# Decay sums of a gated linear attention: one matmul for each of two matrices, against two half-row matmuls with both matrices side by side

## The chip, the cores and the metric

The kernel runs on one core of a Trainium2 chip. The metric is the device time in microseconds (us) of one execution. The engines' names in the profile: PE is TensorE (its weight loads are listed as PEld and overlap its matmuls), DVE is VectorE, ACT is ScalarE, POOL is GpSimd, SP is SyncE, which issues most DMAs.

## The reference

A complex gated linear attention (4 batches, 8 heads, 768 tokens, head size 48) feeds a maxout FFN (model size 384 = 8 x 48, inner size 768) over 3072 tokens.

```python
mag = sqrt(a_re*a_re + a_im*a_im)
scale = minimum(mag, 0.999) / (mag + 1e-6)        # the gate is a*scale: a decay and an angle
for t in range(768):                              # per batch, head
    S = (a_re + 1j*a_im)[t][:, None] * scale[t][:, None] * S + outer(k[t], v[t])
    y[t] = real(q[t] @ S)
x = y as [3072, 384]
out = maximum(maximum(x @ w1, x @ w2), x @ w3) @ w_out
```

The weights arrive as 64-bit floats, everything else as 32-bit floats.

## The kernel before

**Tiles.** The tokens are cut into 24 tiles `x` of 128 tokens, each of two chunks of 64, and 12 groups `g` of two tiles. A tile holds tokens on partitions and the 384 = 8 x 48 channels in columns.

**Decay sums.** `gate_steps` makes `Ln`, minus the logarithm of the clipped magnitude, for each token and channel. `products(x)` needs two sums of it over tokens, both as matmuls with a constant 128x128 matrix of 0, 1 and -1 as stationary operand. `mid` gives each token the signed sum between it and the middle of its block of eight tokens; its entries are nonzero only inside blocks of eight. `rest` gives the sum from that block's middle to the end of the 64-token chunk; it is nonzero only inside a chunk, so both matrices are block-diagonal in 64x64 blocks. The steps of `products`:

- `s0`: the matmul `mds` (L405, PSUM), then E = exp(+mds) and E = exp(-mds) on ACT (L106), multiplied into `k` and `q` (L415; on DVE for the first two groups, on POOL after that).
- `s1`: `k` and `q` times cosine and sine give `Uk` and `Uq` (L420, DVE).
- `s2`, listed as `kt` in `tile_steps`: the matmul `sfx` (L405), En = exp(-sfx) on ACT, and `Uk` times En (L428, DVE). This `Uk` is used for the state update alone.

**The rest of a tile.** `turn` transposes Uk and Uq (`tp`, L442; copies to `K` and `Q` on ACT, L444 and L446). `cut` makes `F`, eight matmuls of a head's 48 channels with 74 columns (L455), and exponentiates it into `f` (ACT, L106). `prep` multiplies `K` and `Q` by columns of `f` into Q's factors, `KB`, `QB` and `QG` (L469, DVE). `scores` makes `A` (L504) and `B` (L507), `gather` copies them by mask into `atm` (L516), `state` makes `dk` (L548) and the running state `g`, `outputs` makes `y` (L576), copied to `xT` (L584). The angles of a group come from `turns`: an arctan (ACT, behind a table load at L109), w times ar and plus ai (L355 and L356, DVE), and the running sums `cs` (PE, L360 and L362).

**The FFN.** `up_step` makes 256 inner channels with one of three weights (`up`, L598). The first is copied to `hT` by ACT (L601), the other two go into `hT` by a maximum on DVE (L603). `out_step` makes `op` (L609).

**PSUM.** `tp`, `F`, `mds`, `sfx`, `cs`, `up`, `y` and `op` share one pool `psM` of four buffers, given out in turn. A matmul therefore waits until the fourth buffer before it has been read.

**Order.** Each engine executes its instructions in program order. `weave` merges lists of steps by fractions of a group: the steps of two tiles, the preparation of the next group (`gate_steps`, both tiles' `s0`, the angles, both tiles' `s1`) and the FFN steps of the tokens that are done. So `s0` of the next group, `mds` in the profile, stands between up steps, and `s2` of the next tile stands before `outputs` of the present one. The steady part is groups 2 and later, from about 180 us on.

**The start.** Constants are made by selects on POOL (`keep`, L120) in `constants_early`, ahead of the first group's gates, and `constants_late`, behind its angles. The weights are loaded as 64-bit words and turned into 32-bit floats by `weight_round` (L284 to L292, DVE and ACT), three rounds before the first angles, the others woven into the first group.

Of the kernel before, what the change touches and what calls it, by code (L numbers as in the profile page):

```python
# [9 lines left out]
FP = mybir.dt.float32  # L10
# [3 lines left out]
AF = mybir.ActivationFunctionType  # L14
OP = mybir.AluOpType
# [30 lines left out]
def kernel(  # L46
# [13 lines left out]
    nc = tc.nc  # L60
    B, H, S, D = q.shape
    P = 128
    L64 = 64
    DD = L64 + D
    DM = H * D
# [23 lines left out]
    nat2 = ctx.enter_context(tc.tile_pool(name="nat2", bufs=2))  # L89
# [4 lines left out]
    psM = ctx.enter_context(tc.tile_pool(name="psM", bufs=4, space=PSUM))  # L94

    T = {}
    order = mybir.DependencyInfo(mybir.DependencyClass.NoSync, mybir.DependencyReason.DATA)

    def tab(ins):

        if "tab" in T:
            tc.add_manual_dep(ins.ins, T["tab"].ins.name, order, reason="table order")
        T["tab"] = ins

    def act(**kw):
        tab(nc.scalar.activation(**kw))  # L106
# [11 lines left out]
    def keep(view, base, pattern, mult):  # L118

        nc.gpsimd.affine_select(out=view, in_=view, compare_op=OP.is_ge, fill=0.0, base=base,  # L120
                                pattern=pattern, channel_multiplier=mult)

    def ones(name, *shape):
        t = const.tile([P, *shape], FP, name=name)
        nc.vector.memset(t, 1.0)
        return t

    def between(view, low, high, lp, hp):

        keep(view, -low - 1, [[-s, n] for s, n in lp], 1)  # L130
        keep(view, high, [[s, n] for s, n in hp], -1)
# [2 lines left out]

    upto = ones("upto", P)

    mid = ones("mid", P)

    rest = ones("rest", P)

    cuts = ones("cuts", NF)

# [11 lines left out]
    fs = [const.tile([P, H, NF], FP, name="f%d" % i) for i in range(2)]  # L154

    def constants_early():
        halves = mid.rearrange("p (n u h) -> p n u h", u=2, h=4)
        left, right = halves[:, :, 0], halves[:, :, 1]
        nc.vector.memset(left, -1.0)
        keep(left, -1, [[-8, 16], [-1, 4]], 1)  # L160
        keep(left, 3, [[8, 16], [0, 4]], -1)
        keep(right, -4, [[-8, 16], [0, 4]], 1)
        keep(right, 4, [[8, 16], [1, 4]], -1)
        keep(upto, 0, [[1, P]], -1)
        make_identity(nc, ident)
        for c in range(2):
            o = L64 * c

            def col(base, n):
                return cuts[:, base + n * c:base + n * c + n]  # L170

            between(col(C8, 4), o + 7, o + 11, [[16, 4]], [[16, 4]])
            between(col(C8B, 4), o + 3, o + 7, [[16, 4]], [[16, 4]])
            vw = col(C16, 4).rearrange("p (n u) -> p n u", u=2)
            between(vw, o + 15, o + 19, [[32, 2], [0, 2]], [[32, 2], [8, 2]])
            vw = col(C32, 8).rearrange("p (i n) -> p i n", i=2)
            between(vw, o + 15, o + 35, [[16, 2], [0, 4]], [[0, 2], [8, 4]])
            vw = col(CK, 8).rearrange("p (n u) -> p n u", u=2)
            between(vw, o + 3, o + 15, [[16, 4], [8, 2]], [[16, 4], [0, 2]])
            between(col(CG, 8), o - 1, o + 3, [[0, 8]], [[8, 8]])  # L180
            between(col(CD, 1), o - 1, o + 63, [[0, 1]], [[0, 1]])

    def constants_late():
        def chunks(dst, f):
            for o in (0, L64):
                nc.vector.tensor_copy(out=dst[o:o + L64], in_=f[o:o + L64, :, o // L64])

        f = nat1.tile([P, 4, 2, L64], FP, tag="e", padded_shape=[P, 6, 2, L64], name="maskf")
        nc.vector.memset(f, 1.0)
        m = f[:, 0].rearrange("p c (n h) -> p (c n) h", h=8)  # L190
        keep(m, 0, [[-8, 16], [0, 8]], 1)
        keep(m, 0, [[8, 16], [1, 8]], -1)
        chunks(maskd.rearrange("p (a t) -> p a t", a=1), f[:, 0:1])
        g = f.rearrange("p i c t -> p (i c t)")[:, 0:4 * L64].rearrange("p (i t) -> p i t", i=4)
        nc.vector.memset(g, 1.0)
        for i, h in enumerate((8, 16, 32, 32)):
            n, w = L64 // h, h if i < 2 else 16
            o = 16 if i == 3 else 0
            m = g[:, i].rearrange("p (n h) -> p n h", h=h)
            keep(m, -o, [[-2 * h, n], [0, h]], 1)  # L200
            keep(m, o + w - 1, [[2 * h, n], [0, h]], -1)
        chunks(masko, g.rearrange("p i (c t) -> p i c t", c=2))
        keep(rest.rearrange("p (n h) -> p n h", h=8), -4, [[-8, 16], [0, 8]], 1)
        keep(rest[:, 0:L64], L64 - 1, [[0, L64]], -1)
        for t in atms:
            nc.gpsimd.memset(t, 0.0)

# [89 lines left out]
    def two(t):  # L297
        n = t.shape[1] // D
        return t.rearrange("p (h u d) -> p h u d", u=1, d=D).to_broadcast([P, n, 2, D])
# [94 lines left out]
    def hd(t):  # L394
        return t.rearrange("p h d -> p (h d)")
# [4 lines left out]
    def products(x):  # L400
        g, c = divmod(x, C)

        def sums(mat, nm):
            ps = psM.tile([P, DM], FP, tag="mm", padded_shape=[P, 512], name=nm)
            nc.tensor.matmul(out=ps, lhsT=mat, rhs=T["Ln", g][:, c * DM:(c + 1) * DM], start=True, stop=True)  # L405
            return ps

        def s0():

            ps = sums(mid, "mds")  # L410
            for nm, sg in (("k", 1.0), ("q", -1.0)):
                E = nat2.tile([P, DM], FP, tag="E", name="E")
                act(out=E, in_=ps, func=AF.Exp, scale=sg)
                eng = nc.gpsimd if g > 1 else nc.vector
                eng.tensor_tensor(out=hd(T[nm, x]), in0=E, in1=hd(T[nm, x]), op=OP.mult)  # L415

        def s1():
            for nm in "kq":
                u = T["U" + nm, x] = us[nm][x % len(us[nm])]
                nc.vector.tensor_tensor(out=u[:, :, :, 0:D], in0=T["CS", x], in1=two(hd(T[nm, x])), op=OP.mult)  # L420

        def s2():

            ps = sums(rest, "sfx")
            En = nat2.tile([P, DM], FP, tag="E", name="En")
            act(out=En, in_=ps, func=AF.Exp, scale=-1.0)
            u = T["Uk", x][:, :, :, 0:D]
            nc.vector.tensor_tensor(out=u, in0=u, in1=two(En), op=OP.mult)  # L428

        return s0, s1, s2  # L430


# [185 lines left out]
    def pre_steps(g, *meanwhile):  # L618
        if g >= NG:
            return []  # L620
        cs = list(range(C))
        parts = [products(g * C + c) for c in cs]
        return gate_steps(g, cs) + [p[0] for p in parts] + [call(angles, g, cs, *meanwhile)] + [p[1] for p in parts]
# [14 lines left out]
    def tile_steps(x):  # L638

        tr, ct, pr = front(x + 1)  # L640
        kt = [products(x + 1)[2]] if x + 1 < NX else []
        return [call(scores, x, "A"), call(gather, x, "A"), call(scores, x, "B")] + tr[:1] \
            + [call(gather, x, "B"), call(state, x)] + tr[1:] + ct + pr[:1] + kt \
            + [call(outputs, x, tokens(x))] + pr[1:]
# [18 lines left out]
    for t in us["k"] + us["q"]:  # L663
        nc.vector.memset(t[:, :, 0, D:], 0.0)
    constants_early()
    for pair in zip(*(gate_steps(0, [c]) for c in range(C))):
        for f in pair:
            f()
    for c in range(C):
        products(c)[0]()  # L670
# [3 lines left out]
    load(1, load_a)  # L674
    angles(0, list(range(C)))
    constants_late()
    for f in [products(0)[1]] + sum(front(0), []) + [products(0)[2], products(1)[1]]:
        f()
# [57 lines left out]
```

## Time and profile before

| | |
|---|---|
| time, median of 6 runs | 728.83 us (726.30 to 729.57) |
| the profiled execution's own time | 729.57 us |
| its span | 727.8 us |
| busy in the span: PE, PEld, DVE | 652.4, 524.3, 518.5 us |
| busy in the span: ACT, POOL | 398.2, 120.8 us |
| mean granted TensorE clock | 0.97 of full speed |
| `mds`: 48 matmul records of 24 matmuls | 24.0 us, mean 584 ns |
| `sfx`: 48 records | 20.6 us, mean 511 ns |
| E: 48 exponentials; En: 24 | 22.2 us, mean 488 ns; 11.8 us, mean 490 ns |

How to read it: a line of groups or of a timeline names the engine, the source line (L405), the operation, output <- inputs, the tile's shape as partitions x elements, and the number of instructions. Busy times are those of the profiled execution. "Idle before" is the engine's idle time just ahead of such instructions, and the name after an arrow says what ended it. A 32-bit matmul shows as two records. Engines work side by side, so their busy times do not add up to the span.

### The profile page before, as it was taken

To read this page: it belongs to the slowest core of one execution; us is meant where nothing else is said; L and a number is where in the kernel's file an instruction comes from. 1 tells how busy PE (TensorE), PEld (TensorE's weight loads), DVE (VectorE), ACT (ScalarE), POOL (GpSimd) and SP (SyncE) were. 2 spreads that over 40 slices of the span, in tenths; PEclk is the share of its full clock that TensorE was granted. 3 is DMA by queue.
4 is the path that set the end of the run, shared out by engine and by line. 5 is a ranking of instruction groups with operands and counts; after the bars stand their busy time and mean duration, and the time that the engine had idled before them with its cause. 6 is when DMAs were issued, how large, how long until landed. Compare 5 with 4: busy or idle time off the path is not lost.

```text
span 727.8 us, 20759 instructions
## 1 busy us (share of the span) xinstructions
PE 652.4 (90%) x9156; PEld 524.3 (72%) x9156; DVE 518.5 (71%) x718; ACT 398.2 (55%) x677; POOL 120.8 (17%) x121
## 2 busy tenths in 40 slices
PE   1356678779999999999999999999999999999998
PEld 0144557657887878878878878868868878878785
DVE  5999988867876876876858768767667778646210
ACT  6778655667557556556566476465565564512000
POOL 9200000601403203103105014013013013000000
PEclk9987799979999999999999999999999999999999
DMA  9790442040320320410410410410410210000000
GB/s 222 213 194 13 97 122 46 13 88 23 55 59 22 63 56 17 88 36 19 93 25 23 88 35 12 89 35 12 89 35 12 46 35 1 2 24 1 14 11 23
DMA packets 134170, 39.10 MB, mean 54 GB/s; under 512 B 126784, under 2 KB 129856, under 8 KB 134080
## 3 DMA queue, kind: packets, MB, share of 16 engines
q1 hardware_dynamic: 133824, 37.76, 23.5%
q8 instruction: 72, 1.18, 0.7%
q14 instruction: 18, 0.15, 0.1%
q10 hardware_dynamic: 256, 0.01, 0.0%
HBM read 33.03 MB, written 4.72 MB: 52 GB/s over the span
## 4 chain that ended last, share of the span: by engine, by line
PE 74%; issue 18%; DVE 3%; ACT 2%; POOL 1%; DMA 1%; SPq 0%; POOLq 0%; ACTq 0%; DVEq 0%
PE up L598 35%; PE op L609 12%; PE y L576 5%; PE tp L442 4%; PE dk L548 4%; PE B L507 3%; PE A L504 2%; PE mds L405 2%; PE sfx L405 2%; PE F L455 2%; PE cs L360 2%; DMA w<-in_moe_w_dram 1%; PE cs L362 1%; POOL ai L338 1%; DMA carry<-nf 0%
## 5 line engine op out<-in xcount | busy, mean ns | idle before, releaser
L598 PE MATMUL up<-xT,w 128*128 128x256 f32 (+1 forms) x1404 | 296.3, 365 | 0.6 <-ACT xT L584 0.6
L598 PEld LDWEIGHTS up<-xT,w 128*128 128x128 f32 x1404 | 247.5, 190 | 38.4 <-DVE hT L603 1.8
L609 PE MATMUL op<-wo,hT 128*128 128x384 f32 x288 | 100.8, 499 | 5.1 <-DVE wo L292 5.1
L603 DVE TENSOR_TENSOR hT<-hT,up 128x512 f32<-128x512 f32 (+1 forms) x78 | 49.9, 641 | 58.1 <-PE up L598 57.2
L338 POOL TENSOR_TENSOR ai<-ai,L 128x768 f32<-128x768 f32 x10 | 25.8, 2580 | 362.3 <-ACT L L106 330.8
L609 PEld LDWEIGHTS op<-wo,hT 128*128 128x128 f32 x288 | 53.2, 191 | 39.1 <-issue 5.8
L469 DVE TENSOR_TENSOR Q<-Q,f 112x512 f32<-112x512 f32 x48 | 41.1, 857 | 41.9 <-ACT f L106 41.9
L444 ACT COPY K<-tp 112x512 f32<-112x512 f32 x48 | 28.0, 583 | 72.6 <-PE tp L442 72.4
L469 DVE TENSOR_TENSOR QB<-Q,f 112x512 f32<-112x512 f32 (+1 forms) x48 | 52.7, 1119 | 0.0
L576 PEld LDWEIGHTS y<-atm,vb 128*32 128x32 f32 x1536 | 39.0, 110 | 13.0 <-issue 7.4
L576 PE MATMUL y<-atm,vb 128*32 128x64 f32 x1536 | 46.4, 222 | 0.0
L548 PEld LDWEIGHTS dk<-vb,uk 128*112 128x112 f32 x384 | 42.8, 183 | 4.6 <-issue 3.3
L576 PE MATMUL y<-QG,g 112*32 112x64 f32 x1536 | 45.8, 220 | 0.0
L548 PE MATMUL dk<-vb,uk 128*112 128x96 f32 x384 | 42.8, 266 | 2.5 <-issue 2.5
L611 ACT COPY ot<-op 128x384 f32<-128x384 f32 x24 | 11.3, 472 | 61.2 <-PE op L609 61.2
L364 ACT ACTIVATE t<-cs 128x384 f32<-128x384 f32 x24 | 11.7, 489 | 58.1 <-PE cs L360 47.3
L507 PE MATMUL B<-QB,KB 112*32 112x80 f32 x1536 | 33.5, 241 | 10.9 <-DVE QB L469 10.9
L405 PE MATMUL mds<-Ln,mid 128*128 128x384 f32 x48 | 24.0, 584 | 20.9 <-POOL cuts L120 15.8
L507 PEld LDWEIGHTS B<-QB,KB 112*32 112x32 f32 x1536 | 29.0, 114 | 17.3 <-issue 8.8
L106 ACT ACTIVATE f<-F 48x296 f32<-48x296 f32 x96 | 39.5, 412 | 1.6 <-PE F L455 0.2
L576 PEld LDWEIGHTS y<-QG,g 112*32 112x32 f32 x1536 | 39.6, 111 | 0.0
L415 POOL TENSOR_TENSOR q<-E,q 128x384 f32<-128x384 f32 x20 | 39.2, 1962 | 0.0
(111 smaller groups left out, 1069.7 us busy)
## 6 DMA issues: line engine op xcount, KB each, us to landing
ar<-in_a_re_dram SPq DMA_DIRECT2D x24, 192.0 KB, 3.8
ai<-in_a_im_dram SPq DMA_DIRECT2D x24, 192.0 KB, 3.9
k<-in_k_dram SPq DMA_DIRECT2D x24, 192.0 KB, 3.2
q<-in_q_dram SPq DMA_DIRECT2D x24, 192.0 KB, 3.0
vb<-in_v_dram SPq DMA_DIRECT2D x96, 48.0 KB, 2.4
out_dram<-ot SPq DMA_DIRECT2D x24, 192.0 KB, 1.9
raw<-in_moe_w_dram SPq DMA_DIRECT2D x5, 768.0 KB, 6.8
raw<-in_moe_w_out_dram SPq DMA_DIRECT2D x3, 768.0 KB, 4.7
```

Source lines behind the costliest of these rows:

```text
L106: tab(nc.scalar.activation(**kw))
L338: (nc.gpsimd if g > 1 else nc.vector).tensor_tensor(out=ai, in0=ai, in1=L, op=OP.mult)
L405: nc.tensor.matmul(out=ps, lhsT=mat, rhs=T["Ln", g][:, c * DM:(c + 1) * DM], start=True, stop=True)
L415: eng.tensor_tensor(out=hd(T[nm, x]), in0=E, in1=hd(T[nm, x]), op=OP.mult)
L442: nc.tensor.transpose(out=tp[0:DD, j], in_=both(T["U" + nm, x], hg * HU + j), identity=ident)
L469: nc.vector.tensor_tensor(out=out, in0=in_, in1=f.to_broadcast([DD, H, 2 * n, 8]), op=OP.mult)
L507: nc.tensor.matmul(out=ps[o:o + 32, h // HU, h % HU * P:h % HU * P + 80], lhsT=T["KB", x][0:DD, h, o:o + 32], rhs=T["QB", x][0:DD, 2 * h + ...
L548: nc.tensor.matmul(out=ps[0:DD, h // HU, h % HU * 96:h % HU * 96 + 96], lhsT=both(T["Uk", x], h), rhs=T["v", x][:, :, h // 2, o:o + D], st ...
L576: nc.tensor.matmul(out=y[32 * (r % 4):32 * (r % 4) + 32, r // 4, c * L64:(c + 1) * L64], lhsT=V[:, c, i, lo:lo + 32] if new else G[0:DD, c ...
L598: nc.tensor.matmul(out=ps[:, j], lhsT=ws[i][:, d, f * P:(f + 1) * P], rhs=xT[:, d], start=(d == 0), stop=(d == KD - 1))
L603: nc.vector.tensor_tensor(out=dst, in0=dst, in1=ps, op=OP.max)
L609: nc.tensor.matmul(out=ps, lhsT=hT[:, f, o:o + P], rhs=wo[:, f], start=(f == 0), stop=(f == KF - 1))
```

## The change

`mid` and `rest` are merged into one constant `sums`. Rows are tokens. Its diagonal 64x64 blocks hold `mid`; the other block of the rows of a chunk holds `rest` of that chunk. A matmul over the 64 rows of one chunk with all 128 columns then gives both sums of that chunk: 64 output partitions with the `mid` sums, 64 with the `rest` sums. So a tile has two matmuls of 64 rows, 128 output partitions and 384 columns, one on the upper and one on the lower row half of the array, each into a PSUM buffer of its own, in place of the two 128-row matmuls `mds` and `sfx`. Both now stand in `s0`. The three exponentials of a tile become six of 64 partitions, since each PSUM buffer holds one chunk; En is made in `s0` too, into buffers of its own, and read from the opposite partition half. `s2` is only the DVE multiplication. The constant takes eight selects of 128x32 and two of 64x64 on POOL, all in `constants_early`, instead of four of 128x64 and, later, two for `rest`.

```diff
-    mid = ones("mid", P)
-    rest = ones("rest", P)
+    sums = ones("sums", P)
...
     def constants_early():
-        halves = mid.rearrange("p (n u h) -> p n u h", u=2, h=4)
-        left, right = halves[:, :, 0], halves[:, :, 1]
-        nc.vector.memset(left, -1.0)
-        keep(left, -1, [[-8, 16], [-1, 4]], 1)
-        keep(left, 3, [[8, 16], [0, 4]], -1)
-        keep(right, -4, [[-8, 16], [0, 4]], 1)
-        keep(right, 4, [[8, 16], [1, 4]], -1)
+        for o in (0, L64):
+            halves = sums[:, o:o + L64].rearrange("p (n u h) -> p n u h", u=2, h=4)
+            left, right = halves[:, :, 0], halves[:, :, 1]
+
+            nc.vector.memset(left, -1.0)
+            keep(left, -1 - o, [[-8, 8], [-1, 4]], 1)
+            keep(left, 3 + o, [[8, 8], [0, 4]], -1)
+            keep(right, -4 - o, [[-8, 8], [0, 4]], 1)
+            keep(right, 4 + o, [[8, 8], [1, 4]], -1)
+        for o, m in ((L64, 0), (0, L64)):
+
+            r = sums[m:m + L64, o:o + L64]
+            nc.vector.memset(r, 1.0)
+            keep(r.rearrange("p (n h) -> p n h", h=8), -4, [[-8, 8], [0, 8]], 1)
...
-        keep(rest.rearrange("p (n h) -> p n h", h=8), -4, [[-8, 16], [0, 8]], 1)
-        keep(rest[:, 0:L64], L64 - 1, [[0, L64]], -1)
...
-        def sums(mat, nm):
-            ps = psM.tile([P, DM], FP, tag="mm", padded_shape=[P, 512], name=nm)
-            nc.tensor.matmul(out=ps, lhsT=mat, rhs=T["Ln", g][:, c * DM:(c + 1) * DM], start=True, stop=True)
-            return ps
-
         def s0():
 
-            ps = sums(mid, "mds")
+
+            pss = []
+            for o in (0, L64):
+                ps = psM.tile([P, DM], FP, tag="mm", padded_shape=[P, 512], name="sums")
+                nc.tensor.matmul(out=ps, lhsT=sums[o:o + L64], rhs=T["Ln", g][o:o + L64, c * DM:(c + 1) * DM],
+                                 start=True, stop=True)
+                pss.append((o, ps))
             for nm, sg in (("k", 1.0), ("q", -1.0)):
                 E = nat2.tile([P, DM], FP, tag="E", name="E")
-                act(out=E, in_=ps, func=AF.Exp, scale=sg)
+                for o, ps in pss:
+                    act(out=E[o:o + L64], in_=ps[o:o + L64], func=AF.Exp, scale=sg)
                 eng = nc.gpsimd if g > 1 else nc.vector
                 eng.tensor_tensor(out=hd(T[nm, x]), in0=E, in1=hd(T[nm, x]), op=OP.mult)
+            En = T["En", x] = nat2.tile([P, DM], FP, tag="En", name="En")
+            for o, ps in pss:
+                act(out=En[o:o + L64], in_=ps[L64 - o:P - o], func=AF.Exp, scale=-1.0)
...
         def s2():
 
-            ps = sums(rest, "sfx")
-            En = nat2.tile([P, DM], FP, tag="E", name="En")
-            act(out=En, in_=ps, func=AF.Exp, scale=-1.0)
             u = T["Uk", x][:, :, :, 0:D]
-            nc.vector.tensor_tensor(out=u, in0=u, in1=two(En), op=OP.mult)
+            nc.vector.tensor_tensor(out=u, in0=u, in1=two(T["En", x]), op=OP.mult)
```

## The prediction

> **What bounds the kernel now.** I read the page's busy line and its slices first:
>
> ```profile
> PE 652.4 (90%) x9156; PEld 524.3 (72%) x9156; DVE 518.5 (71%) x718; ACT 398.2 (55%) x677; POOL 120.8 (17%) x121
> PE   1356678779999999999999999999999999999998
> DVE  5999988867876876876858768767667778646210
> ```
>
> A slice is 18 us. From the tenth on PE is full; in the first nine DVE is. So the change has two prices: in PE time from about 180 us on, and in the chain through DVE and ACT before that. The windows view of one startup stretch and one steady group (columns: length, then PE, PEld, DVE, ACT, POOL busy, clock, DMA share, GB/s) says the same:
>
> ```profile
> 20.00:40.00 20.00, 4.21 (x6) 1.85 (x6) 18.86 (x34) 14.19 (x25) 4.49 (x10) 0.99 0.81 212
> 389.50:442.00 52.50, 52.50 (x755) 42.47 (x756) 39.98 (x52) 31.32 (x54) 9.71 (x6) 1.00 0.23 47
> ```
>
> Next the groups of instructions that the change touches (busy, mean ns | idle before):
>
> ```profile
> L405 PE MATMUL sfx<-Ln,rest 128*128 128x384 f32 x48 | 20.6, 511 | 0.0
> L106 ACT ACTIVATE E<-mds 128x384 f32<-128x384 f32 x48 | 22.2, 488 | 10.2 <-DVE uk L428 5.6 <-PE mds L405 3.5 <-DVE q L415 0.5
> L106 ACT ACTIVATE f<-F 48x296 f32<-48x296 f32 x96 | 39.5, 412 | 1.6 <-PE F L455 0.2
> ```
>
> Last, the timelines of PE, PEld and DVE around the sums of one group (start, length):
>
> ```profile
> 388.73 0.72 PE L455 MATMUL F<-cuts,Ln 128*48 128x74 f32 x16
> 389.38 0.91 PE L405 MATMUL mds<-Ln,mid 128*128 128x384 f32 x2
> 390.13 2.75 PE L598 MATMUL up<-xT,w 128*128 128x256 f32 x12
> 395.93 1.06 PEld L598 LDWEIGHTS up<-xT,w 128*128 128x128 f32 x5 [0.23 <-DVE hT L603]
> 391.21 0.69 DVE L469 TENSOR_TENSOR Q<-Q,f 112x512 f32<-112x512 f32 x1 [1.96 <-ACT f L106]
> 391.82 2.03 DVE L469 TENSOR_TENSOR KB<-K,f 112x1024 f32<-112x1024 f32 x1
> 395.20 0.67 DVE L603 TENSOR_TENSOR hT<-hT,up 128x512 f32<-128x512 f32 x1
> ```
>
> A matmul shows as two records. The reader should see that PE runs gapless, that the one small gate in this window is DVE's hT (it frees the PSUM buffer of the third up), and that DVE idled 1.96 us just before.
>
> **PE, steady part.** A 128x384 sum costs its pitch: 12 op products start at 419.80 and the next thing at 423.77, so 0.33 a record and about 0.65 a matmul. Per group two mds and two sfx go (four of 0.65 = 2.6) and two pairs come. No row of before runs two row halves at once. The nearest is F: eight 74-column matmuls to alternate column halves take 388.73 to 389.38, 0.65, where 74/384 of 0.65 eight times is 1.0. So halves can overlap, and the unknown pair lies between 0.65 (full overlap) and 1.3 (none). I take 0.65, because F is nearer to overlap than to none. A change of shape between neighbours costs something too: up lasts 2.79 behind B and 2.59 in its chain, so I put up to 0.2 on each, and a pair adds one more than the whole matmul did.
>
> The Trainium skill, "TensorE: Matmul & The Clock Gate", on small-K matmuls, gives row tiles that run concurrently and four of them 3.07 times as fast. By that figure (four in 4/3.07 = 1.3 of one) a pair is estimated at some 0.70, and the sum would stay as it is, since PE does not gate the window in which the pairs stand.
>
> In the window from 419 us (second tile of each group) the sfx matmul just disappears: 0.64 off per group (sfx 423.77, y at 424.51, less the shape change), with nothing late behind it: its Q factors are done at 424.05. Ten groups: −6.4.
>
> In the window above, PE by itself would save 0.64 minus two shape changes, about 0.3. But DVE's order changes. The multiplication uk by En now precedes the Q and KB products (into DVE's idle 1.96, free), and the hT of the second up moves behind one more instruction, the first QB. DVE and POOL also exclude each other: KB takes 2.03 while POOL multiplies E into k (391.77 to 392.77), against 1.22 elsewhere, and Q 1.50 against 0.68. E of k now ends when its second half does, 0.38 later, so POOL's k starts at 392.15. By hand: KB 391.82 to 393.04, POOL k to 393.92, Q to 394.46, POOL q to 395.34, QB to 395.9, hT to 396.5, against 395.87 before. That is 0.63 later, less 0.1 because DVE's records overlap (Q's 391.21 + 0.69 is past KB's start at 391.82): the third up's matmul, at 396.15 before, starts at 396.67, +0.52. The window's later waits move with it: the next one, on DVE's w for the angles, has 0.7 to spare. PE would have been ready at 395.83, so the whole saving of this window is turned into a wait. Nine groups: +4.7. Bounds: if hT is in time, −0.3 a group (−2.9 over nine); if the pair takes 1.3, about +0.9 (+8.1).
>
> En is in time: the second tile's sums reuse a buffer that En frees, at about 395.0 (395.40 less PE's saving), and En ends at 393.8 (E from 391.20, six halves of 0.435). A pair holds two of the four buffers of the pool until then; the up behind them takes the other two in turn, the last one freed by hT, which is the gate above. Steady sum: +4.7 − 6.4 = −1.7.
>
> **ACT.** An exponential costs by columns: f on 48 partitions and 296 columns takes 0.412 and E on 128 and 384 takes 0.488 (two in a row 0.87, so 0.435 each). A half is as dear as the whole: per tile six halves for three wholes, 3 x 0.435 = 1.3, 31 us over 24 tiles. In the steady group ACT is busy 31.3 of 52.5; 2.6 more per group lies in its idle time, unless it delays xT or f (f stands ahead of E in ACT's order, so it does not move).
>
> The Trainium skill, "TensorEngine Tiling (Array Packing)", PSUM Bottleneck, warns that "Tiling speeds up TensorE but not PSUM evacuation". By it alone the change would lose all of the 31 us wherever ACT is the bound; the windows say that this is the startup and not the steady part.
>
> **Startup.** Here is what stands in front of the arctan on ACT:
>
> ```profile
> 22.64 0.84 ACT L106 ACTIVATE E<-mds 128x384 f32<-128x384 f32 x2
> 26.14 1.28 ACT L109 ACT_TABLE_LOAD   x1
> 27.43 0.84 ACT L106 ACTIVATE w<-w 128x768 f32<-128x768 f32 x1
> 28.38 0.90 ACT L290 ACTIVATE w<-wo 128x768 f32<-128x768 int32 x1
> ```
>
> Four exponentials (0.42 each) become twelve halves, En's four among them: 8 x 0.42 = 3.4. The weight activation of 28.38 (0.90) now stands ahead of the table load. Together 4.3, so arctan starts at 31.7. DVE follows: it is 18.86 of 20 busy in this stretch and 20.0 of 20 from 60 to 80. Carried through its new order, it idles some 4.1 waiting for k, the masks and w; part is work pulled ahead, so the first gather, at 54.08, starts at 58.2 with 0.5 more done: 3.6 late; 2.9 at the last weight rounds near 95; and uk by En, moved ahead of them, adds 0.87. At 117, when PE gets its first up, it is 3.8, carried on as +4.0. Bounds: 4.5 above (all of the 4.3 and some); 0.5 below, since ACT idles 4.26 from 29.3 on and weight rounds could use DVE's gaps. I take 4.0, near the upper end, as DVE has almost no idle time to give back.
>
> POOL builds the merged constant by ten selects instead of six (0.45 for 128x64 at 5.67): about 1 us more ahead of the first sums at 15.76, which E takes only from 22.64. That slack hides it; without it, +1.
>
> **Sum.** +4.0 − 1.7 = +2.3. The profiled execution took 729.57 (span 727.8 and 1.77 around it), the median of six is 728.83; so 731.9 against the one and 731.1 against the other, rounded to 731.2. About 0.3% is what a measurement of this kernel can tell from no change: 726.6 to 731.0 is "same".
>
> One term I cannot sign: PE stalls inside A at L504 for "issue", 5.8 us in four places late in the span, with no semaphore behind it. Another instruction layout may remove or repeat them, so 2.9 either way is kept for the range.
>
> **Rivals.**
>
> *hT is not the gate* (0.20). If KB and QB run faster than by hand, for instance because POOL's k no longer starts inside KB, hT ends before 395.8 and PE keeps the gain of both windows: nine times 0.96 and once 0.64 is −9.3, with the startup −5.3: 723.5. For it: hT held PE only 0.2 per group before. Against: hT now has one more 0.68 ahead of it. It decides where the first window's up begins before 396.15.
>
> *The halves do not run side by side* (0.17), so the change does not do what it says. A pair takes 1.3, +0.26 a group net, steady about +1.7 instead of −1.7: 4.0 + 1.7 = 5.7, 734.5. For it: no row of before has row halves. Against: F.
>
> *The startup delay is absorbed* (0.20). The table load waits for the exponentials, but DVE fills with weight rounds and the late stretch catches up: +0.5 − 1.7 = −1.2, 727.6; not slower. For it: PE is only half busy before 180 us. Against: DVE at 18.86 of 20.
>
> **How the numbers follow.** The forecast has 0.43, and since it lies just above the bound, 0.33 of that is slower and 0.10 same. The gate-free rival's 0.20 is faster; the halves' 0.17 is slower; the absorbed startup's 0.20 is 0.16 same and 0.04 faster. So faster 0.24, same 0.26, slower 0.50. The range runs from the faster rival, 723.5, to the no-overlap case with half of the A stalls repeated, 734.5 + 2.9, rounded to 737.5. The forecast's own range is 728 to 734.
>
> **What would show it.** Pair: start of the first half to start of the up behind it, about 0.75 if side by side, 1.3 or more if not. Gate: PEld up waiting for hT should grow from 0.2 to over 0.5 per group. Startup: arctan near 31.7, first gather near 58.2, first up near 120.6. The group period should stay within 0.2 of 52.4. A period below 51.7 proves the steady term wrong; an arctan at 31.7 with the first up unmoved proves the startup term wrong.

## The result

The changed kernel takes 730.97 us (median of 27 runs, 727.91 to 734.46) against 728.56 for the kernel before: a ratio of 1.0031, 95% interval 1.0022 to 1.0040, so about 2.3 us slower (1.6 to 2.9). The forecast was 731.2 and the sum said +2.3. The two terms of the sum were each too small, though, and their errors cancelled: the steady part gains 5.6 where 1.7 was forecast (about 2 of it from a stall that the sum had left out), and the start loses 6.5 to 8 where 4.0 was.

The page and the groups of instructions after the change (busy, mean ns | idle before):

```profile
PE 646.0 (89%) x9156; PEld 517.8 (71%) x9156; DVE 518.5 (71%) x720; ACT 435.0 (60%) x749; POOL 115.6 (16%) x125
L414 PE MATMUL sums<-Ln,sums 64*128 64x384 f32 x96 | 26.4, 590 | 30.3 <-POOL sums L120 19.2 <-ACT En L106 5.9 <-DVE Ln L333 4.1
L106 ACT ACTIVATE E<-sums 64x384 f32<-64x384 f32 x96 | 46.5, 484 | 5.2 <-PE sums L414 3.1
```

The sums cost PE 26.4 us instead of 44.6 (mds and sfx together), and the exponentials cost ACT twice what they did: 484 ns for a half, 488 before for a whole.

The timelines of PE, PEld and DVE in a steady group, the same stretch that the prediction showed (5 us later by now):

```profile
393.33 0.72 PE L462 MATMUL F<-cuts,Ln 128*48 128x74 f32 x16
393.98 0.92 PE L414 MATMUL sums<-Ln,sums 64*128 64x384 f32 x4
394.82 2.86 PE L605 MATMUL up<-xT,w 128*128 128x256 f32 x12
...
401.12 8.04 PE L605 MATMUL up<-xT,w 128*128 128x256 f32 x36 [0.65 <-DVE hT L610]
401.12 0.94 PEld L605 LDWEIGHTS up<-xT,w 128*128 128x128 f32 x5 [1.27 <-DVE hT L610]
393.24 0.95 DVE L435 TENSOR_TENSOR uk<-uk,En 128x768 f32<-128x768 f32 x1
395.81 0.69 DVE L476 TENSOR_TENSOR Q<-Q,f 112x512 f32<-112x512 f32 x1 [1.63 <-ACT f L106]
396.42 1.22 DVE L476 TENSOR_TENSOR KB<-K,f 112x1024 f32<-112x1024 f32 x1
397.56 1.50 DVE L476 TENSOR_TENSOR Q<-Q,f 112x512 f32<-112x512 f32 x1
398.98 1.49 DVE L476 TENSOR_TENSOR QB<-Q,f 112x512 f32<-112x512 f32 x1
400.39 0.67 DVE L610 TENSOR_TENSOR hT<-hT,up 128x512 f32<-128x512 f32 x1
...
407.73 0.95 DVE L361 TENSOR_TENSOR w<-w,ai 128x768 f32<-128x768 f32 x1
409.00 1.45 PE L365 MATMUL cs<-w,upto 128*128 128x384 f32 x4
```

A pair takes 0.84 from its start to the up behind it; one whole matmul took 0.75. The third up now waits for hT, 0.65 by its matmul and 1.27 by its weight load, because hT stands behind Q and QB. The waits view (total, times, longest) says that it is so nine times, once a group:

```profile
PEld up L605 <- DVE hT L610: 11.6, 9, 1.4
PE up L605 <- DVE hT L610: 6.0, 9, 0.8
PE A L511 <- issue: 4.1, 3, 1.8
```

And ACT's timeline at the start:

```profile
22.90 1.98 ACT L106 ACTIVATE E<-sums 64x384 f32<-64x384 f32 x4
24.90 0.99 ACT L106 ACTIVATE En<-sums 64x384 f32<-64x384 f32 x2
...
27.25 1.49 ACT L106 ACTIVATE E<-sums 64x384 f32<-64x384 f32 x3
28.77 0.98 ACT L106 ACTIVATE En<-sums 64x384 f32<-64x384 f32 x2
29.77 0.89 ACT L295 ACTIVATE w<-w 128x768 f32<-128x768 int32 x1
30.68 1.28 ACT L109 ACT_TABLE_LOAD   x1
31.97 0.89 ACT L295 ACTIVATE w<-wo 128x768 f32<-128x768 int32 x1
32.77 0.83 ACT L106 ACTIVATE w<-w 128x768 f32<-128x768 f32 x1
```

Twelve halves and two weight activations stand in front of the arctan, where four wholes and one weight activation stood before. It starts at 32.77 instead of 27.43.

To see where the time goes and comes from, take the start of ACT's copy xT of a tile in each trace, and subtract that of the kernel before (us; the names are those of the experiments below):

| tile's xT, before | changed | start new alone (e4) | steady new alone (e10) | steady order mended (e7) | both (e8) |
|---|---|---|---|---|---|
| 218.77 | +5.53 | +7.12 | −0.96 | +5.25 | −0.99 |
| 480.67 (5 groups on) | +4.68 | +7.12 | −1.80 | +1.87 | −4.36 |
| 535.05 (1 group on) | +2.52 | +6.92 | −3.97 | −0.87 | −7.10 |
| 689.21 (last) | +1.11 | +6.96 | −5.80 | −3.50 | −9.70 |

### The profile page after: what moved, and what is told of

The parts are those of the page before. It is cut to its first block, busy times and chain, and to the rows that moved or that the text cites. A ratio compares the mean times of both kernels' runs of the same rounds, so it can differ in the third digit from the quotient of the medians.

```text
span 728.9 us, 20827 instructions
## 1 busy us (share of the span) xinstructions
PE 646.0 (89%) x9156; PEld 517.8 (71%) x9156; DVE 518.5 (71%) x720; ACT 435.0 (60%) x749; POOL 115.6 (16%) x125
## 4 chain that ended last, share of the span: by engine, by line
PE 66%; DVE 6%; issue 5%; ACT 3%; POOL 0%; ACTq 0%; POOLq 0%
PE up L605 33%; PE op L616 12%; PE tp L449 4%; PE dk L555 4%; PE y L583 3%; PE B L514 3%; DVE Q L476 2%; PE A L511 2%; ACT f L106 2%; PE cs L365 2%; PE F L462 1%; DVE KB L476 1%; DVE hT L610 1%; PE cs L367 1%; DVE QB L476 1%
## 5 line engine op out<-in xcount | busy, mean ns | idle before, releaser
L605 PE MATMUL up<-xT,w 128*128 128x256 f32 (+1 forms) x1404 | 302.4, 371 | 6.6 <-DVE hT L610 6.0
L605 PEld LDWEIGHTS up<-xT,w 128*128 128x128 f32 x1404 | 250.3, 195 | 50.8 <-DVE hT L610 12.1
L414 PE MATMUL sums<-Ln,sums 64*128 64x384 f32 x96 | 26.4, 590 | 30.3 <-POOL sums L120 19.2
L106 ACT ACTIVATE E<-sums 64x384 f32<-64x384 f32 x96 | 46.5, 484 | 5.2 <-PE sums L414 3.1
L422 POOL TENSOR_TENSOR k<-E,k 128x384 f32<-128x384 f32 x20 | 30.5, 1527 | 89.9 <-ACT E L106 89.9
L608 ACT COPY hT<-up 128x512 f32<-128x512 f32 (+1 forms) x39 | 21.4, 550 | 29.9 <-PE up L605 29.7
L449 PE MATMUL tp<-ident,uk 128*112 128x128 f32 x192 | 31.6, 291 | 7.6 <-DVE uk L430 7.6
```

Source lines behind the costliest of these rows:

```text
L414: nc.tensor.matmul(out=ps, lhsT=sums[o:o + L64], rhs=T["Ln", g][o:o + L64, c * DM:(c + 1) * DM], start=True, stop=True)
L449: nc.tensor.transpose(out=tp[0:DD, j], in_=both(T["U" + nm, x], hg * HU + j), identity=ident)
L605: nc.tensor.matmul(out=ps[:, j], lhsT=ws[i][:, d, f * P:(f + 1) * P], rhs=xT[:, d], start=(d == 0), stop=(d == KD - 1))
```

## The experiments

Times are medians; each ratio is to the kernel before on the same chip, with its 95% interval.

**e1: hT ahead of QB again.** A no-cost ordering between DVE instructions, and one swap per group is all that it changes:

```diff
-            times(ends, rows8(base[:, :, 16:32]), C16, 4)
+            later(times(ends, rows8(base[:, :, 16:32]), C16, 4), x)   # behind the second up's hT
```

The second QB (C32) and the state's first multiplication get the same.

> The changed kernel, with one pair of DVE instructions swapped in groups 2 and later: hT of the second up stands ahead of QB again, as before the change. My theory (in the steady part the pairs' saving is turned into PE's wait for this hT): PE's wait for hT at up, 11.6 us by the weight loads and 6.0 by the matmuls in the changed kernel, falls below 3 by the loads; the time falls by about 6, from 731.0 to 724.5 to 726, and the group period by 0.6 to 0.8. Rival (the halved sums themselves, or ACT with its doubled exponentials, hold PE, and hT only happens to end last): another wait takes hT's place and the time stays within 1 us, 730 to 732.

Measured: 729.12, ratio 1.0009 (0.9993 to 1.0025): 1.6 to 1.9 less than the changed kernel, not 6. In the traces, xT goes from +6.63 to +5.30 over the five groups of the table, 0.27 a group against 0.17 in the changed kernel. The wait for hT is gone, and another has come, by the waits view:

```profile
PEld up L605 <- DVE hT L610: 0.5, 1, 0.5
PE cs L365 <- DVE w L361: 3.5, 9, 0.4
```

The timelines of ACT and PE show whose it is:

```profile
401.37 2.00 ACT L106 ACTIVATE E<-sums 64x384 f32<-64x384 f32 x4 [0.38 <-PE sums L414]
403.39 0.99 ACT L106 ACTIVATE En<-sums 64x384 f32<-64x384 f32 x2
404.40 1.28 ACT L109 ACT_TABLE_LOAD   x1
...
406.18 0.85 ACT L106 ACTIVATE w<-w 128x768 f32<-128x768 f32 x1
409.63 1.53 PE L365 MATMUL cs<-w,upto 128*128 128x384 f32 x4 [0.39 <-DVE w L361]
```

The second tile's six halves (2.99 us) push back the table load and the arctan, DVE's w comes late, and cs waits. Neither reading was right alone: hT held PE, but w stood just behind it, hidden by the wait for hT.

**e7: w ahead of the next hT as well.** The sum w plus ai, which cs needs, goes ahead of an hT that DVE took first.

```diff
+            later(T["max"], xs[0], "wai")   # this hT behind w plus ai
```

> The changed kernel with hT ahead of QB as in the first experiment, and also w plus ai (what cs waits for) ahead of the hT that stood before it. My theory after the first experiment (two gates stand in a row: hT, then w, which ACT's eight half exponentials push back with the table load and the arctan; taking one away shows the other): PE's wait of cs for w, 3.5 us there, goes below 1, and the time falls by 2 to 4 below the first experiment's 729.1, to 725 to 727. Rival (the arctan on ACT itself is late, whatever DVE's order): cs waits as before, 728.5 to 730.

Measured: 726.51, ratio 0.9959 (0.9944 to 0.9975). PE's wait of cs for w falls from 3.5 to 0.4, and the table's column falls by 3.38 over five groups, 0.68 a group, against 0.17 in the changed kernel. So DVE's order, not the halves as such, cost the steady part 0.5 a group. Before the change both orders were already the ones restored here, so the gain is the pairs' own.

**e6: both matmuls of a pair on the same row half.**

```diff
-lhsT=sums[o:o + L64], rhs=T["Ln", g][o:o + L64, ...]
+lhsT=sums[0:L64],     rhs=T["Ln", g][0:L64, ...]
```

> The changed kernel with both matmuls of a pair on the upper row half (the second one reads the first chunk's rows again, so half of the sums are those of the other chunk). My theory (two row halves run side by side, one row half can't): from the start of a pair to the start of the up behind it 1.3 or more instead of 0.85; two pairs a group add 0.9, of which the wait for hT hides up to 0.7: 2 to 6 slower than the changed kernel, 733 to 737. Rival (the halves did not overlap, and a matmul of 64 rows is just shorter): the pair keeps its 0.85 and the time stays at 731.

Measured: 736.47, ratio 1.0093 (1.0077 to 1.0108), 4.5 more than the changed kernel by the ratios. PE's timeline:

```profile
397.25 1.55 PE L414 MATMUL sums<-Ln,sums 64*128 64x384 f32 x4
398.74 0.48 PE L605 MATMUL up<-xT,w 128*128 128x256 f32 x1
```

1.49 on one row half, 0.84 on two: they run side by side, and a matmul of 64 rows is no shorter than one of 128 (two of those take 1.39, in e5).

**e5: whole matmuls and whole exponentials, the order as changed** (both sums in s0, En early; the two constants of before). The edit in short:

```diff
-for o in (0, L64): ps; matmul(lhsT=sums[o:o + L64], rhs=Ln[o:o + L64]); six Exp of 64 rows
+for mat in (mid, rest): ps; matmul(lhsT=mat, rhs=Ln); three Exp of 128 rows
```

> The changed kernel without halves: both sums by whole 128-row matmuls (mid and rest apart), both in s0, three whole exponentials a tile, En early as in the changed kernel. My theory (halves cost ACT twice, and that is what delays the start; row halves save PE about half a matmul a pair): the arctan comes at 28.5 to 29.5 us instead of 32.8, the first gather about 4 earlier than in the changed kernel; two whole matmuls take 1.3 where a pair took 0.85, which costs 0.2 to 0.5 a group, as the wait for hT hides part. Sum about 729.5, between 728 and 731. Rival (En ahead of the angles is what delays the start, not the halving): the arctan stays behind 31 us, and the time is over 732.

Measured: 729.42, ratio 0.9992 (0.9980 to 1.0003). The timelines of PE in a steady group and of ACT at the start:

```profile
389.69 0.91 PE L414 MATMUL sums<-Ln,mid 128*128 128x384 f32 x2
390.44 0.81 PE L414 MATMUL sums<-Ln,rest 128*128 128x384 f32 x2
391.08 2.75 PE L605 MATMUL up<-xT,w 128*128 128x256 f32 x12
22.93 0.84 ACT L106 ACTIVATE E<-sums 128x384 f32<-128x384 f32 x2
23.67 0.47 ACT L106 ACTIVATE En<-sums 128x384 f32<-128x384 f32 x1
...
26.90 1.28 ACT L109 ACT_TABLE_LOAD   x1
28.20 0.84 ACT L106 ACTIVATE w<-w 128x768 f32<-128x768 f32 x1
```

Two whole matmuls take 1.39; the arctan is back at 28.20. The xT of e5 is 2.8 to 4.0 us late on the first three tiles, up to 136 us, but has that back by 165 us. From 186 to 589 us it stays 0.1 to 0.8 behind that of the kernel before, with no slope, and 2.3 to 2.4 from 610 us on, with longer stalls in A. So En made early is nearly free once the start is over, and the halving is what delays the arctan.

**e4 and e3, e10: one part of the program alone.** e4 makes group 0's sums the new way and all others the old way; e3 and e10 the new way from group 2 on.

```diff
+            if not (g == 0):      # e4;  e3, e10: g > 1;  e2, e9: g > 0
+                ps = whole(mid, "mds")      # the old s0; s2 has the old sfx and En
```

> The other half alone: group 0 the new way, groups 1 and later the old way. My theory: the start's loss alone, 4.0 to 5.8 over the kernel before, 732.6 to 734.4. Rival (the start's delay is absorbed): 728 to 729.5.

Measured: median 736.47, 7.7 more than the kernel before and beyond both ranges; ratio 1.0128 (1.0093 to 1.0163), which two longer executions (739.77 and 743.05) raise. The trace has a rigid shift of 7.1 us from 165 us to 481 us, and 6.9 from there to the end: from 165 us on nothing is given back. POOL also makes the old constants here, and the arctan starts at 33.90, later than in the changed kernel; but the first gather, at 58.63, stands where it stands there (58.62). So does an up that waits for xT (PE's timelines before, changed and e4):

```profile
116.80 2.94 PE L598 MATMUL up<-xT,w 128*128 128x128 f32 x24 [0.57 <-ACT xT L584]
123.05 2.94 PE L605 MATMUL up<-xT,w 128*128 128x128 f32 x24 [0.57 <-ACT xT L591]
123.08 2.94 PE L630 MATMUL up<-xT,w 128*128 128x128 f32 x24 [0.52 <-ACT xT L616]
```

> As the kernel with group 0 the old way, but group 1 goes the old way too, so that the new sums are made from group 2 on, in the steady part alone. My theory (group 0 carries the start's loss; group 1's exponentials are woven among weight rounds and cost little): within 1 us of the kernel with group 0 alone. Rival (DVE and ACT are full until 120 us, so group 1's halves cost as much as group 0's): another 1.5 to 4 faster.

Measured: 726.44, ratio 0.9967 (0.9951 to 0.9982). Its start was still some 2.5 late (first A at 53.04 instead of 50.47), through the experiment itself: a memset of the late-built constant made DVE wait 3.71 behind POOL at 19 us. e10 lets POOL do that memset.

> The third experiment (groups 0 and 1 the old way) again, with the merged constant built by POOL alone and DVE's order left as in the changed kernel: the steady term of the change by itself, with a clean start. My theory: 726.4 less 2.5, 723.5 to 725; that is the kernel before less the steady gain, some 3 to 5. And with both DVE orders it was 719.6, so the two gates together should be worth 4 to 5. Rival (the start's wait was absorbed): 726 to 727.

Measured: 723.40, ratio 0.9923 (0.9900 to 0.9946). That is the change's steady part by itself: −5.6 (−3.9 to −7.3).

**e2 and e9: group 0 alone the old way**, e2 with the late constant's wait, e9 without it.

> The changed kernel, but group 0 (the first two tiles) makes its sums and exponentials the old way; the merged constant is made behind the masks, for group 1 on. My theory (the start loses 4 or more to eight more exponentials ahead of the arctan): the arctan is back at 27.4 us, the first gather near 54.1, and the time falls by 4 to 5.8, to 725.2 to 727. Rival (the delay is made good by 200 us, and the loss lies in the steady part): 730 to 731.

Measured: 732.01, ratio 1.0045 (1.0030 to 1.0059). No gain at all, which spoke against my account of the start. e3, which spares group 1 too, is 5.6 faster, where its theory had within 1 and its rival 1.5 to 4.

> The second experiment (group 0 the old way, the rest the new way) again, with the merged constant built by POOL alone, so that DVE does not stand behind POOL's selects at 19 us. If that wait was the artefact that hid group 0's gain, the time falls by the 2.5 of it, from 732.0 to about 729.5, and group 1's halves cost the other 5 or so against the kernel that spares both groups. If the wait was absorbed, it stays at 731 to 732. If group 1's halves cost nothing, 724 to 725.

Measured: 728.45, ratio 0.9992 (0.9977 to 1.0007). A part of the miss was the artefact (3.9 by the ratios); the rest is group 1: sparing it too (e10) takes off another 5.0 (0.9992 to 0.9923). The prediction had left group 1's halves out. The windows view of 60 to 80 us (as in the prediction), e9 and then e10, shows ACT with 2.2 us more and DVE no longer full:

```profile
60.00:80.00 20.00, 9.30 (x218) 6.03 (x222) 19.30 (x27) 18.35 (x32) 1.03 (x1) 0.76 0.06 11
60.00:80.00 20.00, 9.31 (x234) 6.70 (x238) 20.00 (x28) 16.14 (x25) 1.02 (x1) 0.67 0.06 11
```

**e8: the version that the experiments point to.** New sums from group 2 on, constant by POOL, DVE's two orders as in e7.

> The sums the new way from group 2 on only (as the third experiment), the merged constant built by POOL alone, so that DVE no longer stands 2.5 us behind POOL's selects at 19 us, and both DVE orders of the kernel above. My theory: 726.4 less 2.5 for the start, less 2 to 5 for the two gates: 719 to 722. Rival (the start's artefact is absorbed, or the gates are not additive with it): 724 to 726.

Measured: 719.56, ratio 0.9863 (0.9843 to 0.9883): 10 us faster than the kernel before. Waits of PE in its steady part:

```profile
PE A L538 <- issue: 3.9, 3, 1.4
PE cs L376 <- DVE w L372: 0.4, 1, 0.4
```

## Why the prediction held, and where its steps did not

**The pair**: taken at 0.65 plus a shape change, about 0.75 to the next up; 0.84 measured, and 1.49 without overlap (e6). Right, and the rival in which the halves do not run side by side is out. The Trainium skill, "TensorE: Matmul & The Clock Gate", Part 3, says that row tiles run concurrently; this case agrees, two tiles of 64 rows in 0.84 instead of 1.49.

**The gate of the first window**: forecast +0.52, with −0.64 in the second window, −0.12 a group. Measured −0.17 a group over five groups (5.53 to 4.68). By PE's starts in the group shown, the first window adds 0.48 (F 4.60 late, cs 5.08) and the second takes off 0.64 (op 5.07 late, the y behind it 4.43). The hand replay of DVE named the right instruction and nearly the right size. What it did not see was the second gate: w for cs, which it put 0.7 from trouble. w had slack only because hT held PE by 0.65 (in the changed kernel it ends at 408.68, and cs starts at 409.00): with hT out of the way cs waits (e1). The rival "hT is not the gate" priced both windows at −0.96 a group; taking hT away gave 0.1 more (−0.27), and only with w moved too did it come to −0.68.

**The steady sum**: −1.7 forecast, −5.6 measured (e10). The table's column for e10 parts it: 0.96 by 219 us (the sum had 0.64 there), 0.84 over five groups (0.60), 2.17 in the one group after 481 us, and 1.83 from 535 us to the end. Nearly all of the third is a stall in A that the kernel before has and e10 has not. The timeline of PE before:

```profile
480.97 0.62 PE L504 MATMUL A<-Q,K 112*32 112x48 f32 x35 [1.74 <-issue]
```

The prediction kept this term unsigned and out of the sum. In these traces it goes one way: the profiles with pairs in the steady part (changed, e1, e3 and e6 to e10) have three such stalls (3.6 to 4.9 us together), the three without (before, e4, e5) have four (5.7 to 6.8). Why is not shown; no semaphore stands behind it. So some 2 of the 5.6 came with the pairs' program and not from the terms of the sum. Of the last 1.83, three groups at 0.17 make 0.5 and shorter stalls 0.4 (3.7 against 4.1); some 0.9 stay open.

**The start**: +4.0 forecast; the changed kernel less e10 gives 0.0108, 7.9 by the ratios, and 6.5 in the traces at 219 us. Two terms were too small and one was missing.

- The halves on ACT. From start to start a half takes 0.50 behind another, and a whole 0.37 (e5: two from 22.93 to 23.67). The prediction had halved the length of two wholes in a row (0.84) and taken 0.42 for both. In the timelines the twelve halves take 5.9 and the four wholes of the kernel before 1.5: +4.4 instead of 3.4. With 0.80 for the weight activation (0.90 forecast) and an E that starts 0.26 later, the arctan started at 32.77, not 31.7.
- The way from there to PE. The first gather came at 58.6 (58.2 forecast). But the up at 116.80, which the prediction calls PE's first (ups run from 68.77 on), came at 123.05, not 120.6, and at 123.08 in e4, where only group 0 is made the new way. So group 0 alone makes that up 6.3 late, where the prediction's replay of DVE had 3.8. A wait of DVE for ACT's ex (1.59 us at 113.80 in e4, none at that place before) may be part of it; the rest is open.
- Group 1's halves, which the sum left out.

The terms do not add: group 0 alone costs 7.1 (e4), group 1 alone about 5 (e9 less e10), both together 6.5. The order of the instructions differs in each, and how they share the loss is open. The rival in which the delay is absorbed is out: e4's shift is rigid, though e5 shows that a smaller early delay can be absorbed.

**POOL's constant**: "about 1 us more ahead of the first sums at 15.76" was 3.4 (they start at 19.15, behind two selects that POOL takes after all cuts); the slack up to E hid it. E starts 0.26 later (22.90 against 22.64), but ACT was already 0.23 late at 15.99 and did not wait for the sums.

**ACT as the limit**: 31 us more were counted, 36.8 came (398.2 to 435.0). The Trainium skill, "TensorEngine Tiling (Array Packing)", PSUM Bottleneck, says that after a fourfold speedup of TensorE the copy out of PSUM may become the bottleneck. Here the pair is 1.7 times as fast as two whole matmuls (0.84 against 1.39), and reading its sums by halves delayed the start (e5); in the steady part ACT, with 60% of the span, still set the time of cs in e1, through the order of its work and not its share.

So the total was right by cancellation: a gain too small by 3.9 and a loss too small by 2.5 to 3.9.

## What to carry to other kernels

Two matrices side by side on row halves took PE 0.84 us here instead of 1.39, but each instruction that read a half of the result cost no less than one that read the whole. So look where the reading engine sets the time, and use the new way only where it does not: here from the third group on, for 0.8%, or 1.4% with DVE's order mended as well. When a hand replay shows one wait eating a gain, ask what ends just behind it; two gates can stand so close that taking the first away gives back a fifth of what both cost (0.1 of 0.5 us a group here). And check a sum's terms by switching the change on in each stage alone, since a right total can hide two wrong terms.

## What the runs showed that was not expected

Exponentials of 64 partitions start 0.50 us apart in a row, wholes of 128 partitions 0.37 to 0.39, with the same 384 columns and records of about 0.48 each: the wholes overlap by 0.1 and the halves do not, so that in a row a half is not just as dear as a whole but a third dearer. The exponentials f, on 48 partitions, show the same (0.42 apart, records of 0.41). Why is not shown. The stalls for "issue" inside A (up to 2.0 us each) are four or three according to whether pairs stand in the program, with the same A in it.
